# Mixing by Fourier transform, then a gated feed-forward block: the short column chunk of each batch goes first, and its half-filled row tiles are joined across two batches

## The chip, the cores and the metric

The kernel runs on one core of a Trainium2 chip. The metric is the device time of one execution in microseconds (us). The core has a matrix engine (TensorE, PE in the profile; PEld is its weight load), a vector engine (VectorE, DVE), an activation engine (ScalarE, ACT), a general engine (GpSimd, POOL) and a queue engine (SyncE, SP) that only starts transfers. Each engine takes its instructions in the order of the program, and a semaphore makes one engine wait for another.

## The reference, cut to what matters

```python
X = np.fft.fft(np.fft.fft(x, axis=1), axis=2).real   # x: (8, 3008, 256) float32
t = X.reshape(24064, 256)
out = (gelu(t @ w_gate) * (t @ w_val)) @ w_out       # 256 -> 1536 -> 256, float32 out
```

## The kernel before, in words

**The transform.** For each of the B = 8 batches the 3008 time steps are split as 64 x 47. `fold_x` (POOL, line 208) adds and subtracts channel k and channel 256 - k, `a_step` (line 460, TensorE and ACT) does the short transforms, `z_write` and `z_read` turn the data round through HBM, and `b_steps` (line 498) does the transforms of length 47 in PSUM. Their results are copied into `Y`, a tile of two halves by 1505 columns. A column stands for a frequency. The real spectrum is symmetric, so column c gives two output rows: its own ("plus", even part plus odd part) and that of the mirrored frequency ("minus", even part minus odd part). The copies out of PSUM have two parts: `evac_top` (line 533) writes columns 0 to 767 and `evac_rest` (line 541) columns 768 to 1504.

**The first layer.** The 1505 columns are cut into three chunks, `CH` in line 73: 512, 512 and 481. The loop of line 818 runs over 288 units: batch, chunk, and one of NFC = 12 blocks of 128 hidden features. A unit has five matmuls whose moving operand is the chunk (512 or 481 columns): two for the value (`val_even`, line 597, and `val_odd`, line 628) and three for the gate (`gate_plus`, line 613, and `gate_minus`, line 608, which turns the plus gate into the minus gate in the same PSUM bank after ACT has read it). ACT makes `glp` and `glm` (GELU of the plus and of the minus gate). Two units form a duo. DVE reads the even value into `ev` once per unit, then for a duo at once makes the plus half of `h` (`glp` times value) and `dv`, from which POOL (`minus`, line 647) makes the minus half of `h`. `val_odd` of a unit adds onto the bank that `ev` was read from, so its matmul waits for `ev`. In the first chunk of the first batch there is a second way (`kind` 0, line 571): six matmuls for each unit, and DVE makes both halves.

**The second layer.** `h` is a tile of 128 features by 12 blocks by 1024 columns: plus in columns 0 to 511 and minus, mirrored, in columns 512 to 1023. Two such tiles (`h_tile`, line 132, bufs=2) take turns, so the tile of chunk 2 of a batch lies where that of chunk 0 lay. `l2_steps` (line 659) turns one chunk into a list of matmuls that take 128 columns of `h` as weights and the 256 columns of `w_out` as moving operand, 12 of them for a row tile of 128 output rows. There are 8 row tiles in every chunk. In the 481-column chunk the last plus tile has 97 rows and the last minus tile 96, and each takes 12 matmuls too. That is 24 row tiles and 288 matmuls for a batch, 192 and 2304 in all. Two row tiles share a PSUM bank (`ps_o`, one buffer); `finish` (line 702) has ACT copy it to `osb`, and SP stores it in pieces of 32 rows.

**The order of the work.** It is written out by hand. A chunk's list is queued in `l2q` when its 12 units are over (line 914), and each unit of the next chunk ends with 8 matmuls of it (`second`, line 846): 12 units by 8 use up the 96. The next batch's transform is spread over the units too (lines 809 to 816 and 905 to 913): one `a_step` in each of units 0 to 11, four matmuls of `b_steps` in units 18 to 21, 23 to 26 and 27 to 34, `n_step` (line 434) in unit 22. In batch 0 the `a_step`s stand in units 4 to 13, the first eight steps of `b_steps` in units 21 and 22, `n_step` in unit 23, and eight steps in each of units 24 to 26. Batch 7 has no next batch. POOL's `fold_x` stands in odd units.

Of the kernel before, what the change touches and what calls it, by code (L numbers as in the profile page):

```python
# [10 lines left out]
BF16 = mybir.dt.bfloat16  # L11
AF = mybir.ActivationFunctionType
# [25 lines left out]
def kernel(  # L38
# [20 lines left out]
    nc = tc.nc  # L59
# [10 lines left out]
    NFC = F // 128  # L70
    NCOL = T // 2 + 1
    YW = NCOL + 1
    CH = [(0, 512), (512, 512), (1024, NCOL - 1024)]
    MID = 24

    const_pool = ctx.enter_context(tc.tile_pool(name="const", bufs=1))
# [18 lines left out]
    WNb = const_pool.tile([128, NFC], BF16)  # L95
    WN = const_pool.tile([128, NFC], FP32)
    NQs = [const_pool.tile([128, YW], BF16, name=f"nq{i}") for i in range(2)]
    xf_bufs = [const_pool.tile([128, HJ, 2, 128], BF16, name=f"xf{i}") for i in range(2)]

    Ap = const_pool.tile([128, NG, C], BF16)  # L100
# [397 lines left out]
    def b_steps(b, eo, q):  # L498
# [40 lines left out]
                _sub(ps, [[1, MID], [N2, 8]], 0))  # L539

        def evac_rest():
            ps, Y, g0 = box["ps"], Ys[b], 8 * q
# [12 lines left out]
        if eo == 1 and b == 0:  # L555
            steps += [mm(gi, True) for gi in range(8)]
        def evac():
            evac_top()
            evac_rest()

        return steps, evac, evac_top, evac_rest

# [26 lines left out]

    def layer1(r, ps, W, i, eo, n, start):  # L590
        m = pe.matmul(
# [31 lines left out]
    def plus(r):  # L623
        n = r["n"]
        apart(r["d"]["log"], r["k"], vec.tensor_tensor(
            r["h"][:, r["fc"], :n], r["glp"][:, :n], r["pv"][:, :n], op=ALU.mult))

    def val_odd(u):
        r = banks[u]
        n, nm, d = r["n"], r["nm"], r["d"]  # L630
        if r["kd"] == 0:
            layer1(r, r["pv"], WOM, 1, 1, nm, False)
            hm = _sub(r["h"], [[-1, nm]], r["fc"] * 1024 + 512 + nm - 1)
            apart(d["log"], r["k"], vec.tensor_tensor(
                hm, r["glm"][:, :nm], r["pv"][:, :nm], op=ALU.mult))
            return
        layer1(r, r["pv"], WOP, 1, 1, n, False)
        if r["k"]:
            f = r["fc"] - 1
            apart(d["log"], None, vec.tensor_tensor(  # L640
                r["h"][:, f : f + 2, :n], d["glp"][:, :, :n], d["pv"][:, :, :n], op=ALU.mult))
            d["dv"] = dv_tile()
            apart(d["log"], None, vec.scalar_tensor_tensor(
                d["dv"][:, :, :nm], d["ev"][:, :, :nm], 2.0, d["pv"][:, :, :nm],
                op0=ALU.mult, op1=ALU.subtract))

    def minus(u):
        r = banks.pop(u)
        if r["kd"] and r["k"]:
            nm, d = r["nm"], r["d"]  # L650
            hm = _sub(r["h"], [[1024, 2], [-1, nm]], (r["fc"] - 1) * 1024 + 512 + nm - 1)
            pool.tensor_tensor(hm, d["glm"][:, :, :nm], d["dv"][:, :, :nm], op=ALU.mult)

    def store(b, dst_row, t, p0, s0, ns, rows, step, queue=nc.sync):
        dst = ap_replace(
            out, ap=[[C, rows], [step * C, ns], [1, C]], offset=out.offset + (b * T + dst_row) * C)
        queue.dma_start(out=dst, in_=_sub(t, [[C, ns], [1, C]], s0 * C, p0, rows))

    def l2_steps(b, ci):

        last = (b, ci) == (B - 1, len(CH) - 1)
        c0, n = CH[ci]
        m0 = c0 // 32
        nm = n // 32
        steps = []
        for sign in range(2):
            for pair in range(2):
                box = {}
                for s in range(2):
                    sub = 2 * pair + s  # L670
                    M = min(128, (n if sign == 0 else 32 * nm) - sub * 128)
                    for fc in range(NFC):
                        def run(sign=sign, pair=pair, s=s, sub=sub, M=M, fc=fc, box=box):
                            if last and sign and pair and s and fc == 0:
                                box["ps"] = ps_d()
                            if "ps" not in box:
                                box["ps"] = (ps_o, ps_d, ps_g, ps_g)[
                                    2 * sign + pair if last else 0]()
                            ps = box["ps"]
                            h = hs[(b, ci)]  # L680
                            (pe.matmul(
                                ps[:M, s * C : (s + 1) * C],
                                h[:, fc, sign * 512 + sub * 128 : sign * 512 + sub * 128 + M],
                                Wo_sb[:, fc, :], start=(fc == 0), stop=(fc == NFC - 1)))
                            if last and sign and pair and fc == NFC - 1:
                                finish_half(s, M, box)
                            elif s == 1 and fc == NFC - 1:
                                finish(sign, pair, M, box["ps"])
                        steps.append(run)

        def finish_half(s, M, box):
            if s == 0:
                box["t"] = osb_tile()
            t, ps = box["t"], box["ps"]
            (act.copy, vec.tensor_copy)[s](t[:M, s, :], ps[:M, s * C : (s + 1) * C])
            if s:
                for q in range(4):
                    r0 = 64 * (N2 - (m0 + nm - 1 - 8 - q)) - 32
                    store(b, r0, t, 32 * q, 0, 2 if 32 * q < M else 1, 32, 256,
                          (nc.sync, nc.scalar)[q % 2])  # L700

        def finish(sign, pair, M, ps):
            t = osb_tile()
            if M == 128:
                (act.activation(_sub(t, [[1, 2 * C]], 0), ps, AF.Copy))
            else:
                (act.activation(t[:, 0, :], ps[:, :C], AF.Copy))
                (act.activation(t[:M, 1, :], ps[:M, C:], AF.Copy))
            for q in range(4):
                rb = 8 * pair + q  # L710
                both = rb + 4 < nm
                if sign == 0:
                    m = m0 + rb
                    store(b, 64 * m + (m >= MID), t, 32 * q, 0, 2 if both else 1, 32, 256)
                else:
                    m = m0 + nm - 1 - rb
                    r0 = 64 * (N2 - m) - (32 if m >= MID else 31)
                    if both and m - 4 == 0:
                        store(b, r0, t, 32 * q, 0, 1, 32, 256)
                        store(b, r0 + 256, t, 32 * q, 1, 1, 31, 256)  # L720
                    else:
                        store(b, r0, t, 32 * q, 0, 2 if both else 1, 32, 256)
            if sign == 0 and n % 32 and pair == 1:
                store(b, T // 2, t, n % 128 - 1, 1, 1, 1, 256)

        return steps

# [89 lines left out]
    l2q = []  # L817
    for u in range(NU + 2):
        b, i = divmod(u, PER)
        fills = []  # L820
# [30 lines left out]
        if u == 0:  # L851
# [6 lines left out]
            for e in later_evacs:  # L858
                e()
            n_first(0)  # L860
            act.activation(r["glp"], r["pg"], AF.Gelu)
            plus(r)
        elif u < NU:
            val_even(u)
# [83 lines left out]
```

## Time and profile before

| | |
|---|---|
| time, three runs | 633.71, 634.12, 636.68 us; median 634.12 |
| the profiled execution | 636.08 us; its span, the trace's first to last instruction, 633.9 us, so 2.2 us lie around it |
| granted TensorE clock, mean | 0.997 of full speed |
| weight load (PEld), busy | 410.4 us |
| POOL, busy | 439.7 us |
| moved between HBM and the core | 82.39 MB, 130 GB/s over the span |

Busy time is the sum of the times in which an engine had an instruction running. The times within the trace count from the start of the span.

### The profile page before, as it was taken

To read this page: it belongs to the slowest core of one execution; us is meant where nothing else is said; L and a number is where in the kernel's file an instruction comes from. 1 tells how busy PE (TensorE), PEld (TensorE's weight loads), DVE (VectorE), ACT (ScalarE), POOL (GpSimd) and SP (SyncE) were. 2 spreads that over 40 slices of the span, in tenths; PEclk is the share of its full clock that TensorE was granted. 3 is DMA by queue.
4 is the path that set the end of the run, shared out by engine and by line. 5 is a ranking of instruction groups with operands and counts; after the bars stand their busy time and mean duration, and the time that the engine had idled before them with its cause. 6 is when DMAs were issued, how large, how long until landed. Compare 5 with 4: busy or idle time off the path is not lost.

```text
span 633.9 us, 12988 instructions
## 1 busy us (share of the span) xinstructions
PE 613.4 (97%) x4573; PEld 410.4 (65%) x4628; DVE 541.4 (85%) x654; ACT 477.0 (75%) x971; POOL 439.7 (69%) x448
## 2 busy tenths in 40 slices
PE   4899999999999999999999999999999999999997
PEld 2445666666666666666666666666666666666666
DVE  7688988898888988889888988889888898899992
ACT  7587787877788777877778777786778777776662
POOL 8394987768868687677786688786875555555552
PEclk9899999999999999999999999999999999999999
DMA  8995514553236522565135632456222621211123
GB/s 306 357 269 195 182 48 130 147 198 113 67 109 186 185 88 59 157 183 186 43 90 182 206 112 60 118 167 198 85 68 76 200 55 35 76 49 37 46 51 80
DMA packets 65458, 82.39 MB, mean 130 GB/s; under 512 B 8298, under 2 KB 58986, under 8 KB 62578
## 3 DMA queue, kind: packets, MB, share of 16 engines
q1 hardware_dynamic: 63714, 80.69, 41.4%
q0 software_dynamic: 1552, 0.79, 0.9%
q8 instruction: 36, 0.59, 0.4%
q14 instruction: 28, 0.23, 0.1%
q10 hardware_dynamic: 128, 0.10, 0.1%
HBM read 45.08 MB, written 37.25 MB: 130 GB/s over the span
## 4 chain that ended last, share of the span: by engine, by line
PE 93%; DVE 3%; DMA 1%; ACT 1%; issue 1%; POOL 0%; SPq 0%; ACTq 0%; DVEq 0%
PE ps_o L25 39%; PE ps_g L25 28%; PE ps_v L25 19%; PE ps_d L25 6%; DVE h L25 1%; DMA gate<-z 1%; DVE S L25 0%; DVE dv L25 0%; DMA out_dram<-osb 0%; ACT glp L25 0%; ACT S L25 0%; SPq L25 0%; DVE WOM L25 0%; ACT glm L25 0%; ACT osb L25 0%
## 5 line engine op out<-in xcount | busy, mean ns | idle before, releaser
L25 POOL TENSOR_TENSOR h<-glm,dv 128x1024 bf16<-128x1024 bf16 (+1 forms) x138 | 290.2, 2103 | 170.6 <-DVE dv L25 112.2
L25 PE MATMUL ps_o<-Wo_sb,h 128*128 128x256 bf16 (+2 forms) x2232 | 288.7, 272 | 0.4 <-ACT osb L25 0.3
L25 DVE SCALAR_TENSOR_TENSOR ev<-nq,WN,ps_v 128x512 f32<-128x512 bf16 (+1 forms) x276 | 202.3, 733 | 67.3 <-PE ps_v L25 45.4
L25 PEld LDWEIGHTS <-h 128*128 128x128 bf16 (+2 forms) x2304 | 222.8, 100 | 52.5 <-issue 0.8
L25 ACT ACTIVATE glm<-ps_g 128x512 bf16<-128x512 f32 (+1 forms) x288 | 169.4, 588 | 109.6 <-PE ps_g L25 75.8
L25 DVE TENSOR_TENSOR h<-glp,ps_v 128x1024 bf16<-128x1024 bf16 (+2 forms) x150 | 172.9, 1152 | 4.9 <-ACT glp L25 3.1
L25 ACT ACTIVATE glp<-ps_g 128x512 bf16<-128x512 f32 (+1 forms) x288 | 170.0, 590 | 8.7
L25 DVE SCALAR_TENSOR_TENSOR dv<-ev,ps_v 128x1024 f32<-128x1024 f32 (+1 forms) x138 | 164.4, 1191 | 0.0
L25 POOL TENSOR_TENSOR xf<-xin 128x254 bf16<-128x254 f32 x168 | 118.4, 727 | 0.3 <-DMA xin<-in_x_dram 0.3
L25 PE MATMUL ps_g<-Y,WOP 128*128 128x512 bf16 (+1 forms) x288 | 107.6, 374 | 2.2
L25 PE MATMUL ps_g<-Y,WOM 128*128 128x512 bf16 (+1 forms) x288 | 107.7, 374 | 0.4
L25 PE MATMUL ps_v<-Y,WOP 128*128 128x512 bf16 (+1 forms) x286 | 107.0, 374 | 0.0
L25 PE MATMUL ps_v<-Y,WE 128*128 128x512 bf16 (+1 forms) x282 | 105.7, 375 | 0.0
L25 PEld LDWEIGHTS <-WOP 128*128 128x128 bf16 x576 | 55.7, 97 | 53.6 <-ACT WOP L25 0.4
L25 PE MATMUL ps_g<-Y,WE 128*128 128x512 bf16 (+1 forms) x242 | 90.2, 373 | 0.0
L25 PEld LDWEIGHTS <-WE 128*128 128x128 bf16 x576 | 56.0, 97 | 30.6 <-issue 0.3
L25 ACT ACTIVATE osb<-ps_o 128x512 f32<-128x512 f32 (+2 forms) x107 | 56.5, 541 | 19.2 <-PE ps_o L25 16.6
L25 PEld LDWEIGHTS <-Ap 128*128 128x128 bf16 (+1 forms) x561 | 41.4, 97 | 31.7 <-issue 0.6
L25 ACT ACTIVATE S<-ps_d 128x512 bf16<-128x512 f32 x80 | 47.4, 592 | 0.2 <-PE ps_d L25 0.2
L25 PEld LDWEIGHTS <-G 128*128 128x128 bf16 x213 | 21.4, 102 | 35.4 <-ACT G L25 8.6
L25 ACT ACTIVATE Y<-ps_d 128x192 bf16<-128x192 f32 (+4 forms) x142 | 37.0, 341 | 0.5 <-PE ps_d L25 0.5
L25 PEld LDWEIGHTS <-WOM 128*128 128x128 bf16 x300 | 29.2, 97 | 5.1
(133 smaller groups left out, 243.8 us busy)
## 6 DMA issues: line engine op xcount, KB each, us to landing
out_dram<-osb SPq DMA_DIRECT2D x359, 64.0 KB
xin<-in_x_dram SPq DMA_DIRECT2D x16, 1024.0 KB
Ap<-z SPq DMA_DIRECT2D x24, 512.0 KB
xin<-in_x_dram SPq DMA_DIRECT2D x8, 896.0 KB
z<-S SPq DMA_DIRECT2D x7, 768.0 KB
z<-S SPq DMA_DIRECT2D x8, 512.0 KB
nq<-nrow SPq DMA_DIRECT2D x8, 376.2 KB
z<-S SPq DMA_DIRECT2D x11, 256.0 KB
```

The source lines that it names most:

```text
L25: return lambda *a, **k: self._tc.keep_in_program_order(call(*a, **k))
```

## The change

The 481-column chunk is now chunk 0 of every batch, in place of chunk 2. The copies out of PSUM write columns 768 to 1504 first (`evac_rest` ahead of `evac_top`); at the start of the kernel the top copies of the odd part are the ones put off until the first unit's matmuls are issued.

For this chunk `h` is laid out without a gap: minus in columns 0 to 479, plus in 480 to 960. These 960 columns (without the last, a single row in the middle of the spectrum) are 30 blocks of 32 rows: seven full windows of 128 columns and one half window, columns 896 to 959. The half window is copied by POOL into a tile that is kept: blocks 0 to 7 into `hx`, blocks 8 to 11 into `CW`, a table that is no longer used by then. A batch with an even number fills the left half, the next batch the right half, and only then the two are one row tile. So the list of chunk 0 has 7 row tiles (84 matmuls) in even batches and 8 (96) in odd ones. Its windows are taken in the order 4, 5, 6, 0, 1, 2, 3: plus first.

The single column 960 of chunk 0 goes along with the chunk at columns 0 to 511: when that one's units are over, POOL copies it into column 1023 of the new chunk's `h`, whose value there is a duplicate. The program issues this copy after `minus` of unit 23, in the iteration of unit 24.

Where a list is shorter than 96, the units 6 to 11 of the chunk that works it off take 6 matmuls in place of 8. `finish` has one form for all tiles (one ACT copy of 512 or 256 columns), and the stores follow the blocks. `hs[(b, 2)]`, the tile of chunk 2, still lies where chunk 0's lay.

The diff, cut to its core:

```diff
-    CH = [(0, 512), (512, 512), (1024, NCOL - 1024)]
+    CH = [(1024, NCOL - 1024), (0, 512), (512, 512)]
...
+    HXF = NFC - NCH * 2
+    hx = const_pool.tile([128, HXF, 128], BF16)
...
         def evac():
+            evac_rest()
             evac_top()
-            evac_rest()
...
-            h=hs[(b, ci)], Y=Ys[b], nq=NQs[b % 2])
+            h=hs[(b, ci)], Y=Ys[b], nq=NQs[b % 2], po=0 if n == 512 else 480,
+            mo=512 if n == 512 else 0)
...
+    def windows(b, ci):
+        h = hs[(b, ci)]
+        c0, n = CH[ci]
+        m0, nb = c0 // 32, n // 32
+        ps = [plus_rows(b, m0 + i) for i in range(nb)]
+        ms = [minus_rows(b, m0 + nb - 1 - i) for i in range(nb)]
+        blocks = ps + ms if n == 512 else ms + ps
+        order = range(8) if n == 512 else (4, 5, 6, 0, 1, 2, 3)
+        out = [(h, 128 * w, blocks[4 * w : 4 * w + 4], None) for w in order]
+        if c0 == 0:
+            out[-1] = out[-1][:3] + (b * T + T // 2,)
+        if len(blocks) % 4:
+            left = blocks[-2:]
+            o = 64 * (b % 2)
+            pool.tensor_copy(hx[:, :, o : o + 64], h[:, :HXF, 896:960])
+            pool.tensor_copy(_sub(CW, [[128, NCH * 2], [1, 64]], o), h[:, HXF:, 896:960])
+            if b % 2:
+                out.append((None, 0, st[b - 1]["left"] + left, None))
+            else:
+                st[b]["left"] = left
+        return out
...
             if eo:
-                evac_top()
-                later_evacs.append(evac_rest)
+                evac_rest()
+                later_evacs.append(evac_top)
...
         if 0 < u <= NU and u % 12 == 0:
             pb, pi = divmod(u // 12 - 1, 3)
+            if CH[pi][0] == 0:
+                pool.tensor_copy(hs[(pb, pi)][:, :, 1023:1024], hs[(pb, pi - 1)][:, :, 960:961])
             l2q += l2_steps(pb, pi)
-        second(8 if u <= NU else len(l2q))
+            few = len(l2q) < 96
+        second((6 if few and u % 12 > 5 else 8) if u <= NU else len(l2q))
```

More of the change, by code (lines that the diff above doesn't have):

```diff
@@ L541, in evac_rest @@
         def evac_rest():
+            if Ys[b] is None:
+                Ys[b] = Y_tile()
             ps, Y, g0 = box["ps"], Ys[b], 8 * q
@@ L625, in plus @@
         apart(r["d"]["log"], r["k"], vec.tensor_tensor(
-            r["h"][:, r["fc"], :n], r["glp"][:, :n], r["pv"][:, :n], op=ALU.mult))
+            r["h"][:, r["fc"], r["po"] : r["po"] + n], r["glp"][:, :n], r["pv"][:, :n],
+            op=ALU.mult))
     def val_odd(u):
@@ L632, in val_odd @@
             layer1(r, r["pv"], WOM, 1, 1, nm, False)
-            hm = _sub(r["h"], [[-1, nm]], r["fc"] * 1024 + 512 + nm - 1)
+            hm = _sub(r["h"], [[-1, nm]], r["fc"] * 1024 + r["mo"] + nm - 1)
             apart(d["log"], r["k"], vec.tensor_tensor(
@@ L640, in val_odd @@
             apart(d["log"], None, vec.tensor_tensor(
-                r["h"][:, f : f + 2, :n], d["glp"][:, :, :n], d["pv"][:, :, :n], op=ALU.mult))
+                r["h"][:, f : f + 2, r["po"] : r["po"] + n], d["glp"][:, :, :n], d["pv"][:, :, :n],
+                op=ALU.mult))
             d["dv"] = dv_tile()
@@ L650, in minus, with plus_rows @@
             nm, d = r["nm"], r["d"]
-            hm = _sub(r["h"], [[1024, 2], [-1, nm]], (r["fc"] - 1) * 1024 + 512 + nm - 1)
+            hm = _sub(r["h"], [[1024, 2], [-1, nm]], (r["fc"] - 1) * 1024 + r["mo"] + nm - 1)
             pool.tensor_tensor(hm, d["glm"][:, :, :nm], d["dv"][:, :, :nm], op=ALU.mult)
[L654 to L657, printed above, removed]
+    def plus_rows(b, m):
+        return b * T + 64 * m + (m >= MID), 32
@@ new lines, in minus_rows @@
+    def minus_rows(b, m):
+        return b * T + 64 * (N2 - m) - (32 if m >= MID else 31), 32 if m else 31
+    def windows(b, ci):
[19 more added lines that the diff above has]
+        return out
@@ L659, in l2_steps @@
     def l2_steps(b, ci):
         last = (b, ci) == (B - 1, len(CH) - 1)
-        c0, n = CH[ci]
-        m0 = c0 // 32
-        nm = n // 32
+        ws = windows(b, ci)
         steps = []
[L666 to L689, printed above, removed]
@@ L691, in finish_half, with run @@
-        def finish_half(s, M, box):
+        last_pair = ws[-2:]
+        for w0 in range(0, len(ws), 2):
+            pair = ws[w0 : w0 + 2]
+            box = {}
+            for s, (h, col, _, _) in enumerate(pair):
+                for fc in range(NFC):
+                    def run(w0=w0, pair=pair, s=s, h=h, col=col, fc=fc, box=box):
+                        apart_end = last and w0 == len(ws) - 2
+                        if apart_end and s and fc == 0:
+                            box["ps"] = ps_d()
+                        if "ps" not in box:
+                            box["ps"] = (ps_o, ps_d, ps_g, ps_g)[w0 // 2 if last else 0]()
+                        ps = box["ps"]
+                        if h is not None:
+                            w = h[:, fc, col : col + 128]
+                        elif fc < HXF:
+                            w = hx[:, fc, :]
+                        else:
+                            w = _sub(CW, [[1, 128]], 128 * (fc - HXF))
+                        pe.matmul(
+                            ps[:, s * C : (s + 1) * C], w,
+                            Wo_sb[:, fc, :], start=(fc == 0), stop=(fc == NFC - 1))
+                        if fc == NFC - 1:
+                            if apart_end:
+                                finish_half(s, box)
+                            elif s == len(pair) - 1:
+                                finish(pair, box["ps"])
+                    steps.append(run)
@@ L692, in finish_half, with rows_ap @@
+        def rows_ap(row, n, step=0, ns=1):
+            return ap_replace(out, ap=[[C, n], [step * C, ns], [1, C]], offset=out.offset + row * C)
+        def finish_half(s, box):
             if s == 0:
@@ L694, in finish_half @@
             t, ps = box["t"], box["ps"]
-            (act.copy, vec.tensor_copy)[s](t[:M, s, :], ps[:M, s * C : (s + 1) * C])
+            (act.copy, vec.tensor_copy)[s](t[:, s, :], ps[:, s * C : (s + 1) * C])
             if s:
[L697 to L702, printed above, removed]
-            t = osb_tile()
[L704 to L708, printed above, removed]
-            for q in range(4):
[L710 to L714, printed above, removed]
-                else:
[L716 to L724, printed above, removed]
@@ new lines, in finish_half, with finish, store_pair @@
+                store_pair(last_pair, t, (nc.sync, nc.scalar))
+        def finish(pair, ps):
+            t = osb_tile()
+            ns = len(pair)
+            act.activation(_sub(t, [[1, ns * C]], 0), _sub(ps, [[1, ns * C]], 0), AF.Copy)
+            store_pair(pair, t, (nc.sync, nc.sync))
+        def store_pair(pair, t, queues):
+            ns = len(pair)
+            for q in range(4):
+                rows = [w[2][q] for w in pair]
+                if ns == 2 and rows[0][1] == rows[1][1]:
+                    queues[q % 2].dma_start(
+                        out=rows_ap(rows[0][0], 32, rows[1][0] - rows[0][0], 2),
+                        in_=_sub(t, [[C, 2], [1, C]], 0, 32 * q, 32))
+                else:
+                    for s, (r, n) in enumerate(rows):
+                        nc.sync.dma_start(
+                            out=rows_ap(r, n), in_=_sub(t, [[C, 1], [1, C]], s * C, 32 * q, n))
+            for s, w in enumerate(pair):
+                if w[3] is not None:
+                    nc.sync.dma_start(
+                        out=rows_ap(w[3], 1), in_=_sub(t, [[C, 1], [1, C]], s * C, 127, 1))
@@ L816 @@
     plan = [first | evens, later | evens]
-    l2q = []
+    l2q, few = [], False
     for u in range(NU + 2):
@@ L860 @@
             n_first(0)
-            act.activation(r["glp"], r["pg"], AF.Gelu)
+            act.activation(r["glp"][:, : r["n"]], r["pg"][:, : r["n"]], AF.Gelu)
             plus(r)
```

## The prediction, made before the changed kernel ran

> **What bounds the kernel now.** I read the page first, then the chain of work that ended last in order of time.
>
> ```profile
> span 633.9 us, 12988 instructions
> PE 613.4 (97%) x4573; PEld 410.4 (65%) x4628; DVE 541.4 (85%) x654; ACT 477.0 (75%) x971; POOL 439.7 (69%) x448
> PEclk9899999999999999999999999999999999999999
> PE 93%; DVE 3%; DMA 1%; ACT 1%; issue 1%; POOL 0%; SPq 0%; ACTq 0%; DVEq 0%
> ...
> 275.13 0.87 PE ps_o L25 x8
> ...
> 277.31 0.87 PE ps_o L25 x8
> ...
> 279.26 0.87 PE ps_o L25 x8
> ...
> 281.21 0.87 PE ps_o L25 x8
> ...
> 622.30 2.62 PE ps_d L25 x24
> ```
>
> TensorE is busy 97% of the span, at the full clock, and 93% of the chain is its own work. The lower rows give the beat. The 8 second-layer matmuls that end a unit start at 275.13 and again at 277.31: 2.18 us for a unit that also carries a step of the next batch's transform. From 279.26 to 281.21 it is 1.95 us, a unit that carries none. I call these full and bare units. Eight second-layer matmuls take 0.87 us; the 24 in a row at the end, where nothing else competes, take 2.62 us, or 0.109 us each. So the middle of the kernel is a row of matmuls without gaps, and the question is whether 48 fewer of them still leave a row without gaps.
>
> The page of the Trainium skill "Perfetto Trace Analysis" (§ Identifying the Most-Contended Engine) warns that a high matmul busy share says little about the headroom, and names the weight load's share, here 65%, as a better measure; by that TensorE might wait a third of the time, and 48 matmuls might go and save nothing. The even 0.109 us from one matmul to the next speaks against this reading; it is the last rival below.
>
> **The change part by part.**
>
> *The 48 matmuls.* Does a row tile of 97 rows cost what a full one does?
>
> ```profile
> L25 PE MATMUL ps_o<-Wo_sb,h 128*128 128x256 bf16 x2064 | 268.1, 272 | 0.4 <-ACT osb L25 0.3
> L25 PE MATMUL ps_o<-Wo_sb,h 128*97 128x256 bf16 x84 | 11.5, 273 | 0.0
> ```
>
> Yes: 272 and 273 ns (latencies, which overlap). Before there are 192 row tiles of 12 matmuls, after 188, so 48 matmuls of 0.109 us go: **-5.24 us**. They go in four places only, the units 18 to 23 of batches 0, 2, 4 and 6, which take 6 second-layer matmuls for 8, 0.218 us less a unit. Everywhere else 8 a unit remain.
>
> *Does another engine hold those units up?* Here is DVE's loop, with the matmul that waits for it: in batch 7, where all units are bare, and then in batch 3, with full ones.
>
> ```profile
> 559.13 1.22 DVE L25 SCALAR_TENSOR_TENSOR dv<-ev,ps_v 128x1024 f32<-128x1024 f32 x1
> 560.26 0.74 DVE L25 SCALAR_TENSOR_TENSOR ev<-nq,WN,ps_v 128x512 f32<-128x512 bf16 x1
> 561.24 0.75 DVE L25 SCALAR_TENSOR_TENSOR ev<-nq,WN,ps_v 128x512 f32<-128x512 bf16 x1 [0.23 <-PE ps_v L25]
> 561.91 1.22 DVE L25 TENSOR_TENSOR h<-glp,ps_v 128x1024 bf16<-128x1024 bf16 x1
> ...
> 560.49 2.14 POOL L25 TENSOR_TENSOR h<-glm,dv 128x1024 bf16<-128x1024 bf16 x1 [1.76 <-DVE dv L25]
> ...
> 561.26 0.38 PE L25 MATMUL ps_v<-Y,WOP 128*128 128x512 bf16 x1
> ```
>
> ```profile
> 267.20 1.22 DVE L25 SCALAR_TENSOR_TENSOR dv<-ev,ps_v 128x1024 f32<-128x1024 f32 x1
> 270.41 1.21 DVE L25 TENSOR_TENSOR h<-glp,ps_v 128x1024 bf16<-128x1024 bf16 x1
> 272.68 0.74 DVE L25 SCALAR_TENSOR_TENSOR ev<-nq,WN,ps_v 128x512 f32<-128x512 bf16 x1
> ...
> 268.56 2.14 POOL L25 TENSOR_TENSOR h<-glm,dv 128x1024 bf16<-128x1024 bf16 x1 [0.69 <-ACT glm L25]
> ...
> 274.11 0.38 PE L25 MATMUL ps_v<-Y,WOP 128*128 128x512 bf16 x1
> ```
>
> In a bare duo of 3.90 us the second `ev` ends at 560.26 + 0.74 = 561.00 and the matmul that needs it starts at 561.26: DVE has **0.26 us** to spare, so it can follow a duo of 3.64 us and no faster. In a full duo it ends at 273.42, the matmul starts at 274.11: **0.69 us** to spare. A unit with 6 matmuls is 1.95 - 0.22 = 1.73 us bare and 2.18 - 0.22 = 1.96 us full. In batches 2, 4 and 6 the units 18 to 21 and 23 are full and unit 22 carries `n_step`, which costs more than a step:
>
> ```profile
> 224.93 0.36 PE ps_d L25 x6
> ```
>
> So their duos last 3.9 to 4.1 us, as long as the bare duos that ran without a gap: nothing is lost. In batch 0 the units 18, 19 and 20 are bare (the steps stand in 21 and 22): duo 18/19 would take 3.46 us, DVE needs 3.64, and 20/21 is level with it. Loss 0.2 to 0.4 us; I take **+0.3**.
>
> ACT's loop is the other one: `glp` must be read before `gate_minus` may add onto its bank, and two matmuls less come between them.
>
> ```profile
> 297.30 0.60 ACT L25 ACTIVATE glp<-ps_g 128x512 bf16<-128x512 f32 x1
> ...
> 298.19 0.38 PE L25 MATMUL ps_g<-Y,WOM 128*128 128x512 bf16 x1
> ```
>
> `glp` ends at 297.90, its matmul starts at 298.19; 0.22 us sooner it would start at 297.97, still after. But 0.07 us is little, and in unit 21 of even batches a copy of `Y` and one of `osb` now fall together on ACT. Cost 0 to 0.2 us a unit, at most 24 units; I take 0, from the row.
>
> *The copy of column 960, a new wait.* Chunk 2's `h` lies where chunk 0's lay, and the copy reads chunk 0's. So DVE's first plus write of unit 24 and 25 must wait for POOL's copy, and this stands behind `minus` of units 22 and 23 on POOL. Behind the waiting instruction on DVE stand `dv` and the next `ev`, for which a matmul waits. By the rows of batch 7: `minus` ends at 560.49 + 2.14 = 562.63, the copy takes c, some 0.05 us for the semaphore, and DVE wants to start at 561.91. It is late by c + 0.77; 0.26 of it is to spare, so TensorE loses c + 0.51. By the rows of batch 3: 268.56 + 2.14 + c + 0.05 = 270.75 + c against 270.41, late by c + 0.34, less than the 0.69 to spare as long as c is under 0.35. Units 24 to 26 are full in batches 0 to 6. What is c, for 12 elements in each partition?
>
> ```profile
> L25 POOL CAST xf<-xin 128x4 bf16<-128x4 f32 x84 | 17.3, 205 | 0.0
> L25 POOL CAST TF<-TP 128x48 f32<-128x48 bf16 x1 | 0.2, 236 | 0.0
> L25 POOL CAST wb<-wst 128x1024 bf16<-128x1024 f32 x6 | 6.2, 1040 | 10.9 <-DMA wst<-in_moe_w_val_dram 9.8 <-DMA wst<-in_moe_w_gate_dram 1.1
> L25 POOL COPY col_k<-dv 128x1 f32<-128x1 f32 x1 | 1.1, 1110 | 1.2 <-DVE dv L25 1.2
> ```
>
> Copies of 4 and 48 elements take 205 and 236 ns, but one of a single element took 1110. That one ran beside DVE's folds of the start:
>
> ```profile
> 6.29 1.11 POOL L25 COPY col_k<-dv 128x1 f32<-128x1 f32 x1 [1.21 <-DVE dv L25]
> ...
> 6.15 7.24 DVE L25 TENSOR_TENSOR xf<-xin 128x1016 bf16<-128x1016 f32 x6
> ```
>
> The 84 copies of 4 elements ran in the middle of the kernel, beside the same DVE instructions as the new copy will. I take **c = 0.20**, from the row it is nearest to in size and place, and keep 0.2 to 1.11 for the range. Batch 7 then loses **+0.71 us** once, the others nothing (0.15 us under the limit).
>
> The Trainium skill, "GPSIMD Engine Reference" (§ 1, Specifications), says that POOL shares its SBUF interfaces with VectorE and that they collide with DVE instructions that have two SBUF inputs. The start agrees: the folds read `xin` twice. In the middle, DVE's three instructions read one large operand from PSUM, so by this rule c would be the small one; should they collide there all the same, c is near 1.11 and the sum is that of the first rival.
>
> *The copies of the half window.* 512 and 256 elements in each partition: between the rows of 48 and 1024 elements about 0.6 and 0.4 us on POOL, after `minus` of unit 11. No fold stands in units 12 to 17 in batches 1 to 7; in batch 0 POOL has no `minus` before unit 13. After its 2.14 us POOL waits 1.76 us in a bare duo, which covers them, and the joined tile is read nearly a chunk later. Cost 0; without that cover POOL would be about 1 us late, and `minus` windows are read 36 matmuls, four and a half units, after the chunk's end. In the chunk that gets column 960, the last window alone waits for the copy, seven windows later. Nothing.
>
> *The chunks' new order.* A 481-column chunk is the same work first or last, and where TensorE sets the pace the sum stays. The exception is chunk 0 of batch 0.
>
> ```profile
> 30.10:56.00 25.90, 23.86 (x139) 11.18 (x138) 21.79 (x39) 21.21 (x41) 22.06 (x45) 1.00 0.74 225
> L25 DVE TENSOR_TENSOR h<-glp,ps_v 128x1024 bf16<-128x1024 bf16 x90 | 109.3, 1214 | 0.0
> L25 DVE TENSOR_TENSOR h<-glp,ps_v 128x962 bf16<-128x962 bf16 x48 | 55.4, 1154 | 0.8 <-PE ps_v L25 0.6 <-PE ps_g L25 0.2
> ```
>
> The row by stretches (the first numbers are length and PE busy) has TensorE busy 23.86 of 25.90 us there, so DVE or ACT sets part of the pace. With 31 columns less, a DVE product saves half of 1214 - 1154, 30 ns, 24 times: 0.7 us. TensorE saves 31 of 512 columns of six matmuls of 0.22 us, 0.08 us a unit, 0.9 us. What batch 0 gives back in chunk 2, now 512 wide, is five matmuls instead of six of this: 0.8 us. The sum is -0.1 to +0.2; I take 0.
>
> *Start and end.* The last copy before the first unit's odd part was
>
> ```profile
> 30.25 0.34 ACT Y L25
> ...
> 628.62 1.64 DMA out_dram<-osb
> ```
>
> and is now one of 184 elements in place of 192 in another layout: 0 to 0.3 us, and the copies put off get as much shorter; I take 0. At the end the last stores carry full tiles: the row's transfer has a third more rows at worst in its last piece, I take **+0.1**. The stores stand on SP in the same order with the other transfers, 20 fewer of them in the program's list, and their copies on ACT end up to a unit later once in a chunk: nothing waits for a store but `osb`, two tiles on.
>
> **Sum:** -5.24 + 0.3 + 0.71 + 0.1 = **-4.1 us**. The profiled execution's span goes from 633.9 to 629.8, its time from 636.08 to 632.0. The runs without a profile have a median of 634.12, 1.96 under the profiled one; I carry the difference over: **630.0 us**.
>
> **The rivals.**
>
> *Slower: the copy of column 960 is slow.* Mechanism and place are those of the new wait, once a batch. For c over 0.35 the seven batches with full units lose c - 0.35 each, batch 7 c + 0.51. Level with the rest of the sum (-4.84) is 8c - 1.94 = 4.84, so from **c = 0.85 us** on the kernel is slower. At 1.11, the one `COPY` in the trace, the loss is 7 x 0.76 + 1.62 = 6.9 us: 634.12 + 2.1 = **636.2 us**. For it: it is the only row of the same operation, without a change of type. Against: 84 small casts at 205 ns under the same DVE load.
>
> *The gain is half hidden.* The 0.07 us that ACT has left in the short units isn't enough, or DVE's wait falls in batches 0 to 6 too. Half of the 0.218 us lost in 24 units, 2.6 us: **632.6 us**. For it: both loops have little to spare and ACT's copies move together in unit 21. Against: bare units ran a whole chunk in 1.95 us.
>
> *Nothing is gained: TensorE isn't the limit there* (the reading by the weight load). Then the waits are all that is left, +1.1: **635.2 us**. Against: the beat of 0.109 us.
>
> **How the numbers follow.** Forecast, 630.0 us: 0.68; its own range is 628.8 to 631.0, from the bounds of the terms (batch 0, batch 7 hidden or not, end, ACT at 0.04 a unit). Half hidden, 631.0 to 633.5: 0.18. Nothing gained: 0.06. Slow copy: 0.08, of which half lies over 637.3. The range reaches into the half-hidden case: **628.6 to 632.6**, leaving out about 0.05 below and 0.15 above. 0.5%, about what a measurement of this kernel tells from no change, is 3.17 us: faster is under 630.95, slower over 637.29. Faster: nearly the whole forecast and a little of the half-hidden case, 0.70. Slower: 0.05. Same: 0.25.
>
> **What would show it.** In the changed kernel's trace: 188 x 12 second-layer matmuls; starts of the second-layer groups 1.96 us apart in units 18 to 23 of even batches, with no idle time of PE ahead of `ps_g` there; bare duos of about 3.65 us in units 18 to 20 of batch 0. The plus write of units 24 and 25 waits for POOL in all eight batches, by 0.5 us in seven of them without a gap on TensorE and by 1.0 in the last with a gap of 0.7. The 128x12 copy on POOL at about 0.2 us. It would be wrong if that copy takes over 0.35 us, if the matmul after `glp` waits in the short units, or if POOL's longer queue delays the folds.

## The result and the profile after

The changed kernel takes 632.48 us (median of 10 runs, 631.74 to 634.45), the kernel before 635.53 us (10 runs, 633.71 to 636.68). The ratio is **0.9961, 95% interval 0.9945 to 0.9977**: 0.4% faster, which is less than the 0.5% that counts as faster in the prediction, and 2.5 us above the 630.0 us forecast. The forecast was built on 634.12 us, the median of the three runs of the kernel before that were known then; the ten runs have 635.53, so 1.4 of the 2.5 us lie in the starting value. How much of the forecast saving of 4.1 us came is read from the traces below.

The page of the changed kernel, with its first line, busy times, granted clock and the chain of waits by engine:

```profile
span 630.0 us, 12878 instructions
PE 608.2 (97%) x4522; PEld 402.5 (64%) x4580; DVE 541.7 (86%) x654; ACT 471.8 (75%) x956; POOL 448.7 (71%) x472
PEclk9999999999999999999999999999999999999999
PE 83%; DVE 9%; POOL 3%; ACT 2%; issue 1%; DMA 1%; SPq 0%; DVEq 0%; ACTq 0%; POOLq 0%
```

PEld shows the 48 weight loads that went, 4628 to 4580. The chain that ended last was TensorE's own work for 93% of the span; now it is 83%, and DVE and POOL, off the chain before but for 3%, hold 12%. Something new stops TensorE. (A step on the chain counts with its whole length, so the 12% are not the time lost.)

**Where to measure from.** The two spans differ by 3.9 us, but not all of that is the change. The row by stretches for 24 to 31 us, of the kernel before and then of the changed one (after the busy times: granted clock, DMA share, GB/s):

```profile
24.00:31.00 7.00, 6.90 (x109) 4.54 (x109) 3.27 (x13) 3.49 (x10) 3.80 (x4) 0.76 1.03 405
```

```profile
24.00:31.00 7.00, 6.95 (x117) 4.48 (x117) 3.75 (x14) 5.42 (x14) 4.39 (x5) 1.00 1.04 401
```

In some executions of either kernel the granted clock is halved for part of these 7 us (0.76 is the mean over them), and the profiled one of before was such a one. So I compare from the first `glp` (the GELU of the plus gate, one for each unit) to the end of the span. The timelines of before and of after:

```profile
31.05 0.60 ACT L25 ACTIVATE glp<-ps_g 128x512 bf16<-128x512 f32 x1
```

```profile
29.00 0.58 ACT L25 ACTIVATE glp<-ps_g 128x481 bf16<-128x481 f32 x1
```

633.9 - 31.05 = 602.85 us before, 630.0 - 29.00 = 601.00 us after: **-1.85 us**, where the sum of the prediction was -4.1. The span is printed to a tenth, so a stretch that runs to the end is good to about 0.05 us. Not all of a run's time lies in the span: around it are 2.1 to 2.2 us in every run of the kernel before whose span is on record, and 1.7 to 1.9 in every run of the changed kernel. So another 0.35 us or so went outside the trace, where nothing shows why; the prediction had kept this part as it was.

The starts of `glp` also give the length of every six units:

| six units | before, us | after, us | what lies in it |
|---|---|---|---|
| 18 to 24, batches 2, 4, 6 | 12.70 | 11.46 | 6 matmuls instead of 8 |
| 18 to 24, batch 0 | 12.43 | 11.38 | the same |
| 24 to 30, batches 1 to 6 | 11.97 | 12.69 | 481 columns become 512 (481 in units 0 to 11 instead), and the copy of column 960 |
| 24 to 30, batch 7 | 11.34 | 12.58 | the same |
| a whole batch, 1, 3, 5 | 74.29 | 74.62 | |
| last `glp` to the end | 15.91 | 16.55 | the last list and the last stores |

The short units are there. An odd batch, in which no matmul was saved, is 0.33 us longer: this is new, and the prediction had 0. The waits of DVE in the changed kernel (us in all, times, longest) and the groups of POOL's copies (busy us, mean ns | idle before):

```profile
DVE h L25 <- POOL h L25: 5.2, 7, 0.8
```

```profile
L25 POOL COPY hx<-h 128x512 bf16<-128x512 bf16 x8 | 4.8, 603 | 0.0
L25 POOL COPY CW<-h 128x256 bf16<-128x256 bf16 x8 | 3.2, 394 | 0.0
L25 POOL COPY h<-h 128x12 bf16<-128x12 bf16 x8 | 1.9, 237 | 0.5
```

The copy of column 960 takes 0.24 us; 0.20 was forecast. But DVE waits for it by 0.74 us on the mean, where 0.5 was forecast for all batches but the last. The 7 times are batches 0 to 6 (0.58 us in batch 0, 0.77 or 0.78 in the others). In batch 7 the plus write waits 0.98 us, for the forecast 1.0; the view puts that wait down to TensorE, but the write starts at 595.87, 0.03 us after POOL's copy ends. The chain of waits of the changed kernel in batch 3, in order of time (start, us, what):

```profile
301.08 2.15 POOL h L25
303.24 0.05 issue
303.29 0.25 POOL h L25
303.54 0.02 issue
303.56 1.22 DVE h L25
304.78 1.14 DVE dv L25
305.92 0.04 issue
305.97 0.38 PE ps_v L25
306.34 0.05 PE ps_d L25 x2
```

Read it from the top: `minus` of units 22 and 23, the 12-element copy, DVE's plus write of units 24 and 25 (which overwrites what the copy read), `dv`, and then a matmul onto the bank that `dv` has just freed. In the kernel before this stretch is PE alone.

### The profile page after: what moved, and what is told of

The parts are those of the page before. It is cut to its first block, busy times and chain, and to the rows that moved or that the text cites. A ratio compares the mean times of both kernels' runs of the same rounds, so it can differ in the third digit from the quotient of the medians.

```text
span 630.0 us, 12878 instructions
## 1 busy us (share of the span) xinstructions
PE 608.2 (97%) x4522; PEld 402.5 (64%) x4580; DVE 541.7 (86%) x654; ACT 471.8 (75%) x956; POOL 448.7 (71%) x472
## 4 chain that ended last, share of the span: by engine, by line
PE 83%; DVE 9%; POOL 3%; ACT 2%; issue 1%; DMA 1%; SPq 0%; DVEq 0%; ACTq 0%; POOLq 0%
PE ps_o L25 35%; PE ps_g L25 25%; PE ps_v L25 18%; PE ps_d L25 6%; DVE h L25 4%; DVE dv L25 3%; POOL h L25 2%; DVE ev L25 1%; DMA gate<-z 1%; ACT glp L25 1%; DVE S L25 0%; ACT glm L25 0%; ACT S L25 0%; ACT WE L25 0%; DMA out_dram<-osb 0%
## 5 line engine op out<-in xcount | busy, mean ns | idle before, releaser
L25 PE MATMUL ps_o<-Wo_sb,h 128*128 128x256 bf16 x2136 | 277.7, 272 | 0.4 <-ACT osb L25 0.2
L25 PEld LDWEIGHTS <-h 128*128 128x128 bf16 x2208 | 210.9, 97 | 54.5 <-issue 0.9
L25 PE MATMUL ps_g<-Y,WOP 128*128 128x512 bf16 (+1 forms) x278 | 103.9, 374 | 1.7
L25 PE MATMUL ps_g<-Y,WE 128*128 128x512 bf16 (+1 forms) x249 | 92.9, 373 | 0.0
L25 ACT ACTIVATE osb<-ps_o 128x512 f32<-128x512 f32 x93 | 54.8, 589 | 17.6 <-PE ps_o L25 13.6
L25 ACT ACTIVATE Y<-ps_d 128x192 bf16<-128x192 f32 (+4 forms) x142 | 34.0, 340 | 0.5 <-PE ps_d L25 0.5
```

Source lines behind the costliest of these rows:

```text
L25: return lambda *a, **k: self._tc.keep_in_program_order(call(*a, **k))
```

## The experiments

All times from the first `glp` to the end are called G below.

**The changed kernel once more,** as a yardstick.

> The changed kernel once more, beside the others. Measured from the first GELU of the gate to the end of the span, which leaves the start out: 601.0 us, as in the first profile of it (before: 602.85).

632.47 us (12 runs), ratio 0.9963 (0.9948 to 0.9978), G 601.00, and each stretch of six units outside batch 0 within 0.02 us of the first trace. So differences of 0.03 us in a stretch can be read. In batch 0 the stretches between units 6 and 18 move by up to 0.6 us between executions with the same work there; nothing is read from those.

**Take the new wait away.** Column 960 is kept aside when chunk 0's half window is copied, a whole chunk earlier; the late copy then reads this tile, so nothing that DVE overwrites is still to be read.

```diff
+    cx = const_pool.tile([128, NFC, 1], BF16)
...
+            pool.tensor_copy(cx, h[:, :, 960:961])
...
-                pool.tensor_copy(hs[(pb, pi)][:, :, 1023:1024], hs[(pb, pi - 1)][:, :, 960:961])
+                pool.tensor_copy(hs[(pb, pi)][:, :, 1023:1024], cx)
```

> Column 960 is copied into a tile of its own when chunk 0 ends, twelve units before chunk 2 takes over that chunk's h; the later copy reads the small tile, and DVE's plus write of units 24 and 25 waits for POOL no more. Theory A, this wait holds TensorE up by 0.33 us in each of batches 1 to 6 and 0.85 us in batch 7: 2.8 us less than the changed kernel, 598.2 us from the first GELU to the end, and units 24 to 30 in 12.36 us in place of 12.69. Theory B, these units are longer because of the wider chunk or of ACT's copies, and the wait is hidden: 601.0 us, units 24 to 30 stay at 12.69.

631.27 us (6 runs, 629.93 to 631.51), ratio **0.9933 (0.9915 to 0.9951)**, G 598.34: 2.66 us less than the changed kernel. Units 24 to 30 fall to 12.35 (batches 1 to 6) and 11.72 (batch 7), so the wait had cost **0.34 and 0.86 us** there. The timeline of this kernel at the same place (batch 3):

```profile
302.54 2.14 POOL L25 TENSOR_TENSOR h<-glm,dv 128x1024 bf16<-128x1024 bf16 x1 [0.82 <-DVE dv L25]
304.15 1.21 DVE L25 TENSOR_TENSOR h<-glp,ps_v 128x1024 bf16<-128x1024 bf16 x1
304.74 0.24 POOL L25 COPY h<-cx 128x12 bf16<-128x12 bf16 x1
...
306.41 0.74 DVE L25 SCALAR_TENSOR_TENSOR ev<-nq,WN,ps_v 128x512 f32<-128x512 bf16 x1
...
307.74 0.38 PE L25 MATMUL ps_v<-Y,WOP 128*128 128x512 bf16 x1
```

The plus write now runs ahead of the copy, and TensorE's share of the chain is 92% again. The rows also show what the wait had to work against. `minus` starts 304.15 - 302.54 = 1.61 us before the plus write is due, so with 2.15 for `minus`, 0.05, 0.25 and 0.02 (the chain above) the plus write was 0.86 us late. `ev` ends at 307.15 and its matmul starts at 307.74: 0.59 us to spare, less about 0.05 for the handover (0.04 in the chain). 0.86 - 0.54 = 0.32, and 0.34 was measured. The matmul onto the bank that `dv` frees, the last step of the chain above, has more to spare here (`dv` ends at 306.50, the matmul starts at 307.20), so `ev` sets the loss.

**Make the wait longer.** The 12-element copy is made twice.

```diff
+                pool.tensor_copy(hs[(pb, pi)][:, :, 1023:1024], hs[(pb, pi - 1)][:, :, 960:961])
```

> The changed kernel with the 12-element copy made twice in a row, so that POOL releases DVE about 0.29 us later (0.24 for the copy, 0.05 for the semaphore). Theory A: all of it reaches TensorE in batches 1 to 7, 2.0 us more, 603.0 us from the first GELU to the end. Theory B: 601.0 to 601.3.

636.26 us (12 runs), ratio 1.0003 (0.9989 to 1.0018), G 603.49. Units 24 to 30 go from 12.69 to 12.98 and in batch 7 from 12.58 to 12.88: a second copy adds its whole length, 0.24 and a gap, everywhere. In batch 0, where eight `b_steps` in each of these units had covered the first copy, the second costs 0.3 as well, most of the 0.5 by which G is above what I expected. Two such copies eat the whole gain of the change.

**Put the 48 matmuls back.** The even batches' list gets a row tile more, of 12 matmuls that repeat a window and whose result isn't stored; every unit has 8 again.

```diff
+                out.append(out[-1][:2] + (None, None))
...
+            pair = [w for w in pair if w[2]]
```

> The changed kernel with a twelve-matmul row tile added in even batches that repeats another and is not stored, so that all lists have 96 matmuls and every unit takes 8. 48 matmuls of 0.109 us are 5.2 us. If TensorE alone set the pace of the short units all of it comes back, 606.2 us from the first GELU to the end; by the units 18 to 24 of the two traces (1.24 us in batches 2, 4, 6 and 1.05 in batch 0) 4.8 us, 605.8. If another engine holds these units, under 603.5.

638.7 us (8 runs), ratio 1.0049 (1.003 to 1.0068), G 605.93: 4.93 us more than the changed kernel. In batches 2, 4 and 6 units 18 to 24 take 12.74 and not 11.46, in batch 0 12.46 and not 11.38. The matmuls are worth what the prediction said, -5.24 + 0.3 = -4.94 us.

**Give the kernel before this wait alone.** POOL copies one column of chunk 0's `h` into a tile that nobody reads, at unit 24.

```diff
+            if pi == 1:
+                pool.tensor_copy(cx, hs[(pb, 0)][:, :, 511:512])
```

> The kernel before, with the wait alone: at unit 24, behind minus of units 22 and 23, POOL copies one column of chunk 0's h into a small tile that nobody reads, so that DVE's plus write of units 24 and 25 waits for it. By the rows of before: late by 0.94 us with 0.64 to spare in batches 1 to 6, 0.30 us each; late by 1.15 with 0.29 to spare in batch 7, 0.86; batch 0 nothing to 0.3. Theory A: 2.7 to 3.0 us more than before, 605.5 to 605.9 us from the first GELU to the end, units 24 to 30 in 12.27 in place of 11.97. Theory B, the order of the chunks is what costs: 602.9.

636.4 us (12 runs) against 635.08, ratio 1.0024 (1.0008 to 1.004), G 604.68. Units 24 to 30 go from 11.97 to 12.19 in batches 1 to 6 and from 11.34 to 12.08 in batch 7, less than I expected in the six; batch 0 was shorter by 0.3 in units 6 to 12, which the copy doesn't reach. The copy took 0.195 us here, and before's timeline shows that these 481-column units have 0.64 us to spare, 310.97 less 310.33:

```profile
309.62 0.71 DVE L25 SCALAR_TENSOR_TENSOR ev<-nq,WN,ps_v 128x480 f32<-128x480 bf16 x1
...
310.97 0.36 PE L25 MATMUL ps_v<-Y,WOP 128*128 128x481 bf16 x1
```

The wait costs time without anything else of the change.

**Does the loss hang on the units around the wait?** The prediction had taken its spare time from units with an `a_step` (units 0 to 11); units 24 to 27 carry four `b_steps` matmuls instead. So I put the same kind of wait into the kernel before in two other places: two copies ahead of the plus write of units 0 and 1, where an `a_step` stands in each, and one copy ahead of that of units 12 and 13, which carry nothing.

```diff
+            if pi == 2 and pb + 1 < B:
+                for _ in range(2):
+                    pool.tensor_copy(cx, hs[(pb, 1)][:, :, 511:512])
```

> The kernel before, with two POOL copies of one column of the h tile that chunk 0 of the next batch is about to overwrite, put ahead of the plus write of its units 0 and 1 (batches 1 to 7). Nobody reads their result. Those units carry an a_step each, as the rows did from which the prediction took its 0.69 us. By the rows of before around 255 to 261 us the plus write is late by 2.03 + 0.05 + 0.195 + 0.05 + 0.195 + 0.03 - 1.95 = 0.60 us, and 0.69 less a handover of 0.06 is to spare. My theory (the prediction's rule is right, its mistake was to take the long duos of units 0 to 11 for the duos of units 24 to 27): units 0 to 6 of batches 1 to 6 stay at 13.02 to 13.05, those of batch 7, which carry no a_step, go from 11.72 to 12.4-12.6; first GELU to end 603.6 to 604.0, against 602.85 in before and 604.68 in the run with one copy at unit 24. Rival (a wait of DVE for POOL of this size costs some 0.2 to 0.4 us wherever it stands): units 0 to 6 at 13.2 to 13.4 in all seven, first GELU to end 604.5 to 605.6.

634.34 us (one run), G 603.33. Units 0 to 6 of batches 1 to 6 take 13.02 or 13.03, as before, although DVE waits in each; batch 7, without an `a_step`, goes from 11.72 to 12.45. The timeline of this kernel in batch 3:

```profile
255.29 0.46 POOL L25 COPY cx<-h 128x12 bf16<-128x12 bf16 x2
255.78 1.22 DVE L25 TENSOR_TENSOR h<-glp,ps_v 128x1024 bf16<-128x1024 bf16 x1 [0.41 <-POOL cx L25]
...
258.05 0.74 DVE L25 SCALAR_TENSOR_TENSOR ev<-nq,WN,ps_v 128x512 f32<-128x512 bf16 x1
258.31 2.14 POOL L25 TENSOR_TENSOR h<-glm,dv 128x1024 bf16<-128x1024 bf16 x1 [2.56 <-ACT glp L25]
...
258.98 0.38 PE L25 MATMUL ps_v<-Y,WOP 128*128 128x512 bf16 x1
```

DVE waits 0.41 us (its write is 0.49 late, not the 0.60 that I reckoned), and `ev` still ends at 258.79, 0.19 us before its matmul. The other place:

```diff
+            if pi == 0 and pb:
+                pool.tensor_copy(cx, hs[(pb - 1, 2)][:, :, 480:481])
```

> The kernel before, with one POOL copy of one column of the h tile that chunk 1 is about to overwrite, put ahead of the plus write of units 12 and 13 (batches 1 to 7). Nobody reads its result. These units carry no step, so their duo is the short one. By the rows of before around 279 to 286 us the plus write is late by 2.14 + 0.05 + 0.195 + 0.03 - 1.41 = 1.0 us, and 0.26 less a handover of 0.06 is to spare. My theory: units 12 to 18 go from 11.79 to 12.5-12.6 in batches 1 to 6 and from 11.71 to 12.5 in batch 7, first GELU to end 602.85 + 7 x 0.8 = 608.3 to 608.6. Rival (a wait of this kind costs the 0.2 to 0.4 us that it cost at unit 24): units 12 to 18 at 12.0 to 12.2, first GELU to end 604.5 to 605.6.

640.79 us (one run), G 608.10. Units 12 to 18 go from 11.79 to 12.48 to 12.51 in batches 1 to 6 and from 11.71 to 12.43 in batch 7: **0.70 us a time**, a little under the 0.8 of my theory, and far over the rival's 0.2 to 0.4. The timeline:

```profile
285.19 0.20 POOL L25 COPY cx<-h 128x12 bf16<-128x12 bf16 x1
285.39 0.38 PE L25 MATMUL ps_v<-Y,WE 128*128 128x512 bf16 x1
285.43 1.22 DVE L25 TENSOR_TENSOR h<-glp,ps_v 128x1024 bf16<-128x1024 bf16 x1 [0.82 <-POOL cx L25]
```

One rule holds in all four places: loss = lateness of the plus write - (spare time - 0.05). The lateness is taken against the run of the same units without a wait (before's trace, or that of the early copy), set to the same start of a `glp`: for units 12 and 13, before's plus write starts 283.00 - 279.29 = 3.71 us after the `glp` of unit 12, that of the run 285.43 - 280.81 = 4.62. So the table tests the step from lateness to loss. The lateness reckoned before these runs was 0.09 to 0.14 us too large (0.60, 0.94 and 1.0 for 0.49, 0.80 and 0.91).

| place | late, us | spare, us | by the rule | measured |
|---|---|---|---|---|
| units 0 and 1, two copies | 0.49 | 0.69 | 0 | 0 |
| units 24 and 25, before with one copy | 0.80 | 0.64 | 0.21 | 0.22 |
| units 24 and 25, changed kernel | 0.86 | 0.59 | 0.32 | 0.34 |
| units 12 and 13, one copy | 0.91 | 0.26 | 0.70 | 0.70 |

**The end.** From the last `glp` to the end the changed kernel takes 0.64 us more, and 0.1 was forecast. Two suspects: DVE's or ACT's last copy waits for an `osb` tile that a store still reads, or the last stores themselves are longer. Both runs start from the kernel with the early copy. The first gives the last pair a tile of its own:

```diff
-                box["t"] = osb_tile()
+                box["t"] = work.tile([128, 2, C], FP32, tag="ev", bufs=2, name="osl")
```

> The early-copy kernel, whose last pair of row tiles is copied into a tile of its own (the place of ev, free by then) instead of an osb buffer whose stores are still under way. If the wait of ACT's last copy for those stores (0.76 us later than its matmuls) makes the end longer, the stretch from the last gate GELU to the end goes from 16.5 back to about 15.9 us, and 0.6 us are gained; if the fuller stores are what is longer, it stays at 16.5.

631.68 us (6 runs), ratio 0.994 (0.9921 to 0.9958); last `glp` to the end 16.46, against 16.50 with the shared tile. The wait is gone from ACT, and nothing is won: DVE's copy, which waits for TensorE's last matmul anyway, is later. The second leaves out the store of 32 rows, so that the last stores move as many rows as before:

```diff
+                if short and q == 3:
+                    queues[1].dma_start(
+                        out=rows_ap(rows[0][0], 32), in_=_sub(t, [[C, 1], [1, C]], 0, 96, 32))
+                    continue
```

> The early-copy kernel without the last 32 rows of the last row tile (they are computed and not stored), so that the last piece carries 32 KB as before and not 64. If the fuller store makes the end longer, 16.5 goes to about 15.9 us from the last gate GELU to the end; if not, 16.4 to 16.5.

631.78 us (one run); last `glp` to the end 16.18. DVE's last copy in before, in after and in this run:

```profile
630.25 0.42 DVE L25 COPY osb<-ps_d 96x256 f32<-96x256 f32 x1 [8.68 <-DMA out_dram<-osb]
```

```profile
625.77 0.42 DVE L25 COPY osb<-ps_d 128x256 f32<-128x256 f32 x1 [8.58 <-DMA out_dram<-osb]
```

```profile
625.84 0.42 DVE L25 COPY osb<-ps_d 128x256 f32<-128x256 f32 x1 [8.58 <-PE ps_d L25]
```

From its end to the end of the span (633.9, 630.0 and 629.7) are 3.23, 3.81 and 3.44 us. So the 32 rows account for 0.3 to 0.4 of the 0.6; 0.1 to 0.2 us between the last copy and the end stays unexplained, and the answer lay between what the two theories expected.

## Why the prediction was wrong, point by point

| step | forecast, us | measured, us | from |
|---|---|---|---|
| 48 matmuls, with what batch 0 loses | -4.94 | -4.93 | all 192 back, against the changed kernel |
| the copy of column 960 | +0.71 | +2.66 | the changed kernel, against the early copy |
| the end | +0.1 | +0.64 | last `glp` to the end |
| order, half-window copies and the rest | 0 | -0.22 | what is left to the -1.85 |
| sum | -4.1 | -1.85 | G |

**The matmuls: right.** An `h` window of 97 rows cost what a full one does, and the gain came through whole. The starts of the second-layer groups in batch 2 of the changed kernel, units 18 to 21:

```profile
212.66 0.82 PE L25 MATMUL ps_o<-Wo_sb,h 128*128 128x256 bf16 x6
214.50 0.82 PE L25 MATMUL ps_o<-Wo_sb,h 128*128 128x256 bf16 x6
216.35 0.81 PE L25 MATMUL ps_o<-Wo_sb,h 128*128 128x256 bf16 x6
218.18 0.82 PE L25 MATMUL ps_o<-Wo_sb,h 128*128 128x256 bf16 x6
```

They lie 1.83 to 1.85 us apart, not the forecast 1.96, and the reason is the mistake of the next paragraph: these units too were counted with the surcharge of an `a_step`. Their duos of 3.69 us come close to the 3.64 that DVE can follow, but hold. Bare units 18 and 19 of batch 0 took 1.73 + 1.97 = 3.70 us for the forecast 3.65. In the sum two small misses cancel, so the agreement to 0.01 us is in part luck: the loss in batch 0 came out as 1.31 - 1.08 = 0.23 for the forecast 0.3, and ACT's 0.07 us to spare was all but enough: 1.28 of 1.31 us were gained in each of the other even batches.

The rival "nothing is gained" leaned on the Trainium skill, "Perfetto Trace Analysis" (§ Identifying the Most-Contended Engine), which has TensorE's headroom judged by the weight load's busy share, beside a second measure that was not worked out here. Read by that share alone, 65% would leave room. The runs disagree: 4.93 of 5.24 us were won. The distance from one matmul to the next was the better witness.

**The new wait: right in mechanism, place and price of the copy, wrong in what was there to cover it. This is the step that failed:** "By the rows of batch 3: [...] late by c + 0.34, less than the 0.69 to spare as long as c is under 0.35. Units 24 to 26 are full in batches 0 to 6." The prediction knew two kinds of unit, full (2.18 us) and bare (1.95), and put every unit with a step of the transform into the first. But the rows of batch 3 that it used come from units with an `a_step`, two matmuls of 256 columns. Units 24 to 27 carry four matmuls of 47 columns. The chain of waits of the kernel with the early copy shows what such a unit lasts when nothing stops it:

```profile
300.31 0.87 PE ps_o L25 x8
...
302.04 0.05 PE ps_d L25 x2
302.09 0.22 PE ps_g L25
302.31 0.05 PE ps_d L25 x2
302.36 0.88 PE ps_o L25 x8
...
304.41 0.87 PE ps_o L25 x8
```

Two of these matmuls take 0.05 us, so a unit lasts 2.05 us and a duo 4.10, where the prediction reckoned with 4.36. The shorter duo counts twice: the plus write is due 0.24 us sooner after `minus` (1.61 and not 1.85), which with a copy of 0.24 instead of 0.20 and gaps of 0.07 instead of 0.05 makes it 0.86 us late and not 0.54; and 0.59 us are to spare, not 0.69. The loss was called nothing in six batches, and was 0.34 in each, 2.0 us in all, most of the 2.3 by which the sum was off. Batch 7 lost 0.86 for the forecast 0.71. (These make 2.9; the 2.66 of the table hold 0.3 less from the early units of batch 0, which move from run to run.) The waits at units 0 and 12 show that the rule itself was sound, and that in units with an `a_step` the forecast "nothing" would have come true.

In the prediction's list this is the second half of the rival "half hidden": DVE's wait falls in batches 1 to 6 too. Its time, 632.6 us, is the one that came, and that is luck: it was reckoned as half of the gain of 24 short units, which was not lost, and from the starting value of 634.12 us. The rival "slow copy" fell: 0.24 us, not 1.11. The Trainium skill, "GPSIMD Engine Reference" (§ 1, Specifications), has POOL collide, on the SBUF interfaces that they share, with DVE instructions that have two SBUF inputs or run in a two-port mode. In the changed kernel the copy can't test this, since DVE stood waiting while it ran. In the kernel with the early copy it ran beside the plus write, which has one large operand in SBUF, and took 0.24 us as well; beside the folds at the start, which have two, a copy took 1.11. The traces agree with the Trainium skill here.

**The copies of the half window: right.** 0.60 and 0.39 us, and units 12 to 18 take 11.79 us before and after. **The order of the chunks: right** where it can be read. An odd batch is longer by 0.33 us, all of it the wait: with the early copy it takes 74.29 us, as before. Batch 0 is 1.55 us shorter, 1.08 of it the matmuls; the rest is within what batch 0 moves from run to run, together with the -0.1 to +0.2 that was forecast. **The start: right** as far as it can be seen: the first `glp` at 29.0 and 29.3 us in executions at full clock, 30.9 to 31.8 in the others, in the runs built on either kernel. **The end: too small,** +0.64 for +0.1, a part of it not settled. The 20 fewer stores of the prediction are a miscount without effect: both traces have 400.

The kernel with the early copy beats both. In the same series on the same chip it has 631.27 us, the changed kernel 632.47 and the kernel before 635.40. Its runs have 2.1 to 2.2 us around the span, as before, so of its 2.66 us in G some 0.35 are lost again outside the trace.

## What to carry to other kernels

When a wait is weighed against spare time, take both from the very units in which the wait falls, with the same extra work in them, and redo the sum if the units differ: 0.13 us a unit turned a cover that held into one that failed six times over. A copy that must read a tile before it is reused makes the writer of the next round wait for all that stands ahead of the copy on its engine, however short the copy is (here `minus`, 2.15 us, ahead of 0.25); read the value out when it is made, and the wait is gone.

## What the runs showed of the hardware

In some executions TensorE's granted clock is halved for 3.4 us near the start. The row by stretches of the kernel before:

```profile
24.16:27.56 3.40, 3.40 (x34) 1.83 (x32) 0.85 (x3) 1.25 (x3) 0.89 (x1) 0.50 1.05 420
```

Seven of the eleven traces have such a fall, each to 0.50 for 3.4 us, from 23.3 us at the earliest to 28.4 at the latest; in the other four it stays full there. The DMA engines are as busy without it (shares of 1.03 and 1.04 above). What differs is how long TensorE had just waited for the DMA of `gate`, in before and after:

```profile
23.60 2.67 PE L25 MATMUL ps_d<-G,gate 128*128 128x512 bf16 x7 [2.35 <-DMA gate<-z]
```

```profile
23.03 1.90 PE L25 MATMUL ps_d<-G,gate 128*128 128x512 bf16 x8 [1.78 <-DMA gate<-z]
```

It is 2.29 to 2.72 us in the seven traces and 1.78 to 2.11 in the four. That the longer wait brings on the fall is suggested by this and not shown; no run changes the wait alone. Runs with a mean clock of 0.998 or less have medians of 636.29 us (before, 23 runs) and 634.22 (after, 8), those with 0.999 or more 634.49 (20) and 632.08 (14): about 2 us, as much as the change itself brought. Within each group the change is worth 2.1 to 2.4 us, which is the 1.85 of the traces and the 0.35 around them. Five of the six runs with the early copy have the lower clock, so its median understates it.

A matmul of 47 columns (183 ns of latency) comes out every 0.025 us, so four of them cost a tenth of a microsecond, less than half of what two of 256 columns do (0.22).
